# Batching a kernel's 16-bit low products over three blocks of tokens, with the convolution cut by block

## The chip, the cores and the metric

The program runs on one core of a Trainium2 chip. A core has a matrix engine (TensorE, PE in the profile, with its weight loads shown apart as PEld), three further engines (VectorE or DVE, ScalarE or ACT, GpSimd or POOL), a queue that only issues transfers (SyncE or SP), and 16 DMA engines that carry the transfers of all queues. The metric is the device time of one execution in microseconds (us); a number of executions is summed up by its median.

## The reference

An input of 8 sequences of 4096 tokens with 192 features is convolved along the tokens, causally, with 7 taps; the taps are a softmax over 7 weights of each of 8 heads, and a head owns 24 features. The result goes through a two-layer network with a squared ReLU:

```python
w = np.exp(weight - np.max(weight, axis=-1, keepdims=True))
w = w / (np.sum(w, axis=-1, keepdims=True) + 1e-09)           # 8 heads x 7 taps
out = np.einsum('hk,bskhg->bshg', w, x_unf)                    # x_unf: the last 7 tokens
x = out.reshape(32768, 192)
h = x @ w_in                                                   # 192 -> 2048
r = np.maximum(h, 0.0)
g = s * (r * r) + b
return (g @ w_out).astype(np.float32)                          # 2048 -> 192
```

All is float32.

## The kernel before

**Tiling.** The 32768 tokens are 32 super-blocks `n` of 1024 tokens, each of two blocks `j` of 512. The hidden layer of 2048 is 8 pairs `p` of 2 x 128. One step is `(n, j, p)`; there are 16 steps to a super-block. The 192 features are cut into features A (the first 128) and features B (the other 64). The 64 rows of features B of both blocks of a super-block lie above each other in one tile of 128 rows, so one convolution of 512 columns serves both blocks.

**Precision.** TensorE multiplies in a rounded 32-bit format, so every operand is held as a high part and a low part, and the products high x high, low x high and high x low are summed. For convolved features the parts are the two halves of `sA` (features A) and the rows of `tB` (features B). `wA` and `wB` hold the same rows with the upper and lower 64 exchanged; each is made by two DMAs on the SP queue (`swap`, L254 to L258), so that two products on 64 rows each can run side by side on the 128 rows of the array.

**One step on TensorE.** `first(n, j, p)` (L659 to L677) makes 18 products of 64 rows, in pairs, into a PSUM tile `h`: six with `sA`, six with `tB` and `wB`, and last six with `wA`. ScalarE applies ReLU (L684) and squares (L691), VectorE rounds the square to `qh` (L693), and subtracts to get the low part, for `n >= 3` scaled and in 16 bits (`half_lows`, L720 to L729). `second(n, j, p)` then makes the 12 products of `qh` with the output weights. `second` runs two steps behind `first` (LAG), and one more for the first pair of a block; so `second(n, j, 7)`, which ends a block, comes after `first` of step 1 of the next block.

**The low products.** The 16-bit low parts are not multiplied step by step. They wait in a ring of places (`place`, RING = 18 of them) and are multiplied when a block ends. For features A (L829) that is done at the end of every block, on 64 rows, two side by side. For features B (`lows_B`, L783) each product uses 128 rows and 64 columns, two side by side on different columns. They are done for two blocks at once: at the end of a block with `j = 0` they are held, and at the end of `j = 1` the held block's go into a fresh PSUM tile `late` (out of the pool of `h`), the other's into its accumulator. VectorE then adds `late` to the held output tile `oH` (L867).

**Outputs.** At the end of a block ScalarE empties four accumulators into `oA`, `oA2`, `oB`, `oB2` (L843, L846). The rest are DMAs on the POOL queue, in its order: `oB2` is added to `oB` (L858), `oA2` to `oA` (L859), the lower rows of each finished `oB` to its upper rows (L872), and the results go to memory (L875). Each of these waits for the landing of the one that it builds on.

**The convolution ahead.** VectorE convolves features with one instruction a tap (L247 for the first, L249 for the other six), as a list of steps that a generator yields: 7 taps of A for block 0, two of splitting (the ScalarE copy L264; the subtraction L266 with the swap), 7 taps of B, three of splitting B, then A for block 1: 28 steps a super-block. `convolve(k)` advances it by k steps at the end of a step, as the tables CONV and PARTS say. `scale` (L222) sets the taps of a super-block from the peak of its inputs: VectorE reduces (L171, L178, L180, L181), GpSimd multiplies the taps (L228). It is called at the last step of a super-block for the one after the next.

**What sets the order.** The instructions of a step are traced in the order above. A scheduling layer places them on each engine's queue and adds the semaphores; each queue then runs in its order.

## Time and profile before

| what | value |
|---|---|
| median of 3 runs (lowest, highest) | 2040.69 us (2040.59, 2041.22) |
| profiled execution: its own time, its span | 2040.5 us, 2038.6 us |
| PE, busy share of the span | 100%, 18404 products |
| PEld, DVE, ACT, POOL, busy share | 80%, 82%, 65%, 18% |
| mean granted TensorE clock | 1.000 |
| DMA, mean rate | 75 GB/s |

The span runs from the first instruction to the last; the 1.9 us between it and the execution's own time lie around it. A share is an average over the whole span: the first 93 us (super-block 0, with the weights unpacked on the side) differ from the rest. In a timeline row the columns are start in us, duration in us, engine, source line, operation, written tile<-read tiles, shape, count, and in brackets the idle time before it with what ended it. Several products of one kind stand in one row, and since they overlap in pairs, a row's duration runs past the start of the next; distances are read from start to start.

### The profile page before, as it was taken

The numbers are of one execution on the slowest core, as the hardware profiler recorded it, in microseconds if no ns is written. First come the engines' busy times: TensorE is split into PE (matmuls) and PEld (weight loads), VectorE is DVE, ScalarE is ACT, GpSimd is POOL, SyncE is SP. The second block draws the span as 40 slices with busy tenths as digits, with TensorE's granted clock in tenths as the row PEclk, the third lists the DMA queues.
The fourth block names the chain that finished last, engine by engine and source line by source line (L and its number), as shares of the span: only waits on it lengthen the run. The fifth ranks groups of instructions, "written<-read, shape, count | busy, mean of one in ns | idle before, by whom it ended". The sixth has DMA issues, their size and how long they took to land.

```text
span 2038.6 us, 43011 instructions
## 1 busy us (share of the span) xinstructions
PE 2029.5 (100%) x18404; PEld 1632.9 (80%) x18404; DVE 1676.4 (82%) x2232; ACT 1329.8 (65%) x1444; POOL 372.3 (18%) x471
## 2 busy tenths in 40 slices
PE   9999999999999999999999999999999999999999
PEld 6788887877877878778778788787787787887876
DVE  9888988878888878888788888788887888887864
ACT  8878866666666666666666666666666666666665
POOL 0012121112221112211122211122112122112210
PEclk9999999999999999999999999999999999999999
DMA  5023332233332323332333323233323333332321
GB/s 197 21 53 92 79 87 71 64 76 79 81 76 71 71 68 81 84 74 60 73 82 86 76 71 68 71 81 81 74 63 73 81 87 72 73 68 68 71 63 30
DMA packets 60080, 152.82 MB, mean 75 GB/s; under 512 B 11120, under 2 KB 11376, under 8 KB 59888
## 3 DMA queue, kind: packets, MB, share of 16 engines
q0 software_dynamic: 32160, 66.90, 16.1%
q1 hardware_dynamic: 27584, 83.04, 15.2%
q8 instruction: 144, 2.36, 0.6%
q14 instruction: 48, 0.39, 0.2%
q10 hardware_dynamic: 144, 0.13, 0.0%
HBM read 35.57 MB, written 25.20 MB: 30 GB/s over the span
## 4 chain that ended last, share of the span: by engine, by line
PE 96%; DVE 3%; ACT 0%; issue 0%; DMA 0%; SPq 0%; DVEq 0%
PE h L669 47%; PE acc L803 33%; PE acc L829 10%; PE acc L783 3%; PE h L783 3%; DVE ql L698 1%; DVE c L415 0%; DVE t L401 0%; DVE accA L249 0%; DVE W L421 0%; DVE t L398 0%; DVE W L423 0%; DVE t L394 0%; DVE c L414 0%; DMA xA<-in_xA 0%
## 5 line engine op out<-in xcount | busy, mean ns | idle before, releaser
L684 ACT ACTIVATE q<-h 128x1024 f32<-128x1024 f32 x496 | 506.7, 1022 | 415.5 <-PE h L669 414.6
L693 DVE CAST qh<-q 128x1024 fp32r<-128x1024 f32 x477 | 330.1, 692 | 304.1 <-ACT q L691 297.6
L691 ACT ACTIVATE q<-q 128x1024 f32<-128x1024 f32 x512 | 543.8, 1062 | 14.2
L803 PE MATMUL acc<-qh,W 64*128 64x512 f32 x3960 | 513.5, 376 | 0.0
L669 PE MATMUL h<-sA,W 64*128 64x512 f32 x3072 | 427.5, 384 | 2.6 <-DVE W L423 1.7
L803 PEld LDWEIGHTS acc<-qh,W 64*128 64x128 f32 x3960 | 374.9, 186 | 52.5
L669 PE MATMUL h<-wA,W 64*128 64x512 f32 x3072 | 415.6, 376 | 0.0
L669 PE MATMUL h<-wB,W 64*128 64x512 f32 x1536 | 413.6, 376 | 0.0
L669 PE MATMUL h<-tB,W 64*128 64x512 f32 x1536 | 413.6, 376 | 0.0
L726 DVE TENSOR_TENSOR ql<-q,qh 128x1024 f16<-128x1024 f32 x260 | 328.8, 1265 | 9.0
L669 PEld LDWEIGHTS h<-sA,W 64*128 64x128 f32 x3072 | 290.5, 186 | 52.0 <-DVE W L423 2.5
L669 PEld LDWEIGHTS h<-wA,W 64*128 64x128 f32 x3072 | 291.1, 186 | 40.8
L669 PEld LDWEIGHTS h<-tB,W 64*128 64x128 f32 x1536 | 285.4, 186 | 27.3 <-issue 0.2
L803 PE MATMUL acc<-qh,WB 64*128 64x512 f32 x1980 | 299.9, 376 | 0.0
L669 PEld LDWEIGHTS h<-wB,W 64*128 64x128 f32 x1536 | 285.4, 186 | 13.6
L249 DVE SCALAR_TENSOR_TENSOR accA<-xA,taps,accA 128x512 f32<-128x512 f32 x348 | 261.0, 750 | 6.2
L803 PEld LDWEIGHTS acc<-qh,WB 64*128 64x128 f32 x1980 | 187.4, 186 | 26.2
L726 DVE TENSOR_TENSOR words<-q,qh 128x1024 f16<-128x1024 f32 x154 | 194.7, 1264 | 5.3
L829 PEld LDWEIGHTS <-words 64*128 64x128 f16 x1852 | 85.5, 94 | 115.0 <-issue 19.1
L858 POOL DMA_DIRECT2D oB<-oB x60 | 61.6, 1026 | 538.9 <-ACT oB L846 514.0
L249 DVE SCALAR_TENSOR_TENSOR accB<-xB,taps,accB 128x512 f32<-128x512 f32 x174 | 129.9, 747 | 2.2
L843 ACT ACTIVATE oA<-acc,bias,v 128x512 f32<-128x512 f32 x57 | 44.5, 781 | 123.4 <-PE acc L829 123.4
(169 smaller groups left out, 1687.1 us busy)
## 6 DMA issues: line engine op xcount, KB each, us to landing
wA<-sA SPq DMA_DIRECT2D x126, 256.0 KB, 3.7
wB<-tB SPq DMA_DIRECT2D x60, 256.0 KB, 5.1
oB<-oB POOLq DMA_DIRECT2D x60, 256.0 KB, 3.3
oA<-oA POOLq DMA_DIRECT2D x60, 256.0 KB, 3.7
outT<-oA POOLq DMA_DIRECT2D x60, 256.0 KB, 2.3
xA<-in_xA SPq DMA_DIRECT2D x24, 515.0 KB, 3.6
xB<-in_xB SPq DMA_DIRECT2D x32, 259.0 KB, 2.8
oB<-oB POOLq DMA_DIRECT2D x60, 128.0 KB, 2.7
```

What stands on the lines that cost most here:

```text
L249: nc.vector.scalar_tensor_tensor(acc, src, w[:, k : k + 1], acc, op0=ALU.mult, op1=ALU.add)
L669: nc.tensor.matmul(h[:, i, :], w_in(w, p, chunk[0], rows), folded(chunk[part]), start=start, stop=stop,)
L684: nc.scalar.activation(q, h, AF.Relu, scale=scale)
L691: nc.scalar.activation(q, q, AF.Square)
L693: cast(qh, q)
L698: nc.vector.tensor_tensor(ql, q, qh.bitcast(F32), op=ALU.subtract)
L726: nc.vector.tensor_tensor(ql.rearrange("p f (b a) -> p f b a", a=2), *(v.rearrange("p f (a b) -> p f b a", a=2) for v in (q, qh.bitcast(F3 ...
L783: nc.tensor.matmul(to[k * DB :][0:DB], halves[1][:, 2 * p + k, :], ql[:, k, :], start=start and p == 0, stop=p == NPAIR - 1, skip_group_ch ...
L803: nc.tensor.matmul(accs[to + 2 * i], w(f, r), folded(q[r, f % 2, :]), start=start and f == 0, stop=stop and f == ends[i],)
L829: nc.tensor.matmul(accs[2 * i], halves[0][r, f, :], low[r], start=False, stop=f == ends[i],)
L843: nc.scalar.activation(o[k], accs[k], AF.Identity, scale=sb, bias=0.0 if early else bias[:, k : k + 1])
L858: nc.gpsimd.dma_start(o[1], o[3], accum_op=ALU.add)
```

## The change

- `BATCH = 3`: low products of features B are held for two blocks and done at the end of the third, counted over all scaled blocks, whether `j` is 0 or 1. Both halves of `late` are used, for two held blocks, and VectorE adds both (L867 before, L903 in the changed file).
- `RING = 26`: eight more places, in a tile `more` of their own.
- To make room: `sA` and `wA` have two buffers, not three. `tB` and `wB` become one tile for each block (`tB0`, `tB1`, `wB0`, `wB1`), each with one buffer, not two.
- The convolution's steps from super-block 2 on come block by block (`steps_by_block`): B (7 taps and the rounding), then for each block A (7 taps), `split_B` of that block with its own swap, and `split_A`. There are 28 steps as before. Block 0 is `begun` after 18.
- `scale` is called for super-block `n + 1` at step `(n, 0, 2)`, not for `n + 2` at `(n, 1, 7)`.
- PARTS has a row for blocks that start a batch and one for others; the first super-blocks have a table BEGIN.

The diff, without the places that only follow a new name:

```diff
@@ -28,14 +28,28 @@
 WARM = (BLK, BLK // 2, BLK // 2)
-GAP = 136
+GAP = 128
 SCALED = 3
-RING = 18
-PARTS = (1, 5, 2, 1, 1, 2, 1, 1), (2, 3, 0, 2, 1, 2, 2, 2)
+RING = 26
+BATCH = 3
+PARTS = (
+    ((2, 3, 3, 1, 2, 2, 1, 1), (2, 4, 0, 2, 1, 2, 1, 1)),
+    ((1, 4, 3, 2, 1, 2, 1, 1), (1, 7, 0, 1, 1, 1, 1, 1)),
+)
+BEGIN = {
+    (1, 0): (3,) * 8,
+    (1, 1): (1,) * 8,
+    (2, 0): (2, 1, 2, 2, 1, 2, 1, 2),
+    (2, 1): (2, 2, 2, 2, 2, 1, 1, 1),
+    (3, 0): (2, 2, 2, 2, 2, 2, 2, 1),
+    (3, 1): (2, 2, 2, 2, 2, 2, 1, 0),
+}
 EXPONENT = 0x7F800000
...
@@ -222,7 +236,7 @@
             m = greatest(self.peaks, 1)
-            v = small.tile([P, 3], F32, name="v")
+            v = small.tile([P, 3], F32, name="v", bufs=4)
             powers(m, v[:, 0:1], v[:, 1:2], -40)
@@ -259,8 +273,8 @@
         def split_A(self, j, acc):
-            s = self.sA[j] = xs.tile([P, 2, BLK], F32R, name="sA", bufs=3)
-            self.wA[j] = xs.tile([P, 2, BLK], F32R, name="wA", bufs=3)
+            s = self.sA[j] = xs.tile([P, 2, BLK], F32R, name="sA", bufs=2)
+            self.wA[j] = xs.tile([P, 2, BLK], F32R, name="wA", bufs=2)
             nc.scalar.copy(s[:, 0, :], acc)
@@ -269,42 +283,38 @@
             yield
-        def split_B(self, acc):
-            self.tB = xs.tile([P, 2, BLK], F32R, name="tB")
-            self.wB = xs.tile([P, 2, BLK], F32R, name="wB")
-            hiB = xs.tile([P, BLK], F32R, name="hiB", bufs=1)
-            nc.vector.tensor_copy(hiB, acc)
-            yield
-            for j in range(2):
-                r = slice(j * DB, (j + 1) * DB)
-                nc.vector.tensor_copy(self.tB[0:DB, j, :], acc[r, :])
-                nc.vector.tensor_tensor(
-                    self.tB[DB:P, j, :], acc[r, :], hiB[r, :].bitcast(F32), op=ALU.subtract
-                )
-                if j == 1:
-                    self.swap(self.wB, self.tB)
-                    self.begun = True
-                yield
+        def places_B(self, j):
+            self.tB[j] = xs.tile([P, BLK], F32R, name=f"tB{j}", bufs=1)
+            self.wB[j] = xs.tile([P, BLK], F32R, name=f"wB{j}", bufs=1)
+            return self.tB[j], self.wB[j]
+        def split_B(self, j, acc, hiB):
+            r = slice(j * DB, (j + 1) * DB)
+            t, w = self.places_B(j)
+            nc.vector.tensor_copy(t[0:DB, :], acc[r, :])
+            nc.vector.tensor_tensor(
+                t[DB:P, :], acc[r, :], hiB[r, :].bitcast(F32), op=ALU.subtract
+            )
+            self.swap(w, t)
...
@@ -320,14 +330,19 @@
             r = slice(i * HB, (i + 1) * HB)
-            b = (self.tB, self.wB) if i == 0 else (self.wB, self.tB)
+            b = (self.tB[j], self.wB[j]) if i == 0 else (self.wB[j], self.tB[j])
             return (
                 (i, self.sA[j][r, 0, :], self.sA[j][r, 1, :]),
                 (1 - i, self.wA[j][r, 0, :], self.wA[j][r, 1, :]),
-                (2, b[0][r, j, :], b[1][r, j, :]),
+                (2, b[0][r, :], b[1][r, :]),
             )
         def steps(self):
+            if self.n == 1:
+                return self.steps_begin()
+            return self.steps_by_block()
+        def steps_begin(self):
             for j in range(2):
@@ -335,7 +350,27 @@
                     yield from self.conv(acc, self.xB, self.tapB, BLK)
-                    yield from (self.split_B_at_once if self.n == 1 else self.split_B)(acc)
+                    yield from self.split_B_at_once(acc)
+        def steps_by_block(self):
+            accB = xs.tile([P, BLK], F32, name="accB", bufs=1)
+            yield from self.conv(accB, self.xB, self.tapB, BLK)
+            hiB = xs.tile([P, BLK], F32R, name="hiB", bufs=1)
+            nc.vector.tensor_copy(hiB, accB)
+            yield
+            for j in range(2):
+                acc = xs.tile([P, BLK], F32, name="accA")
+                yield from self.conv(acc, self.xA[:, j * BLK :], self.tapA, BLK)
+                self.split_B(j, accB, hiB)
+                yield
+                split = self.split_A(j, acc)
+                next(split)
+                yield
+                next(split)
+                self.begun = True
+                yield
         def conv_tensor(self, acc, diag, x, taps=range(K)):
@@ -709,11 +743,13 @@
                 more = more.rearrange("p k c -> p (k c)")
-            elif k < RING - 2:
+            elif k < 16:
                 more = wordp.tile([P, CT, 2], I32, name="words").bitcast(F16)
                 more = more.rearrange("p f w -> p (f w)")
+            elif k < 18:
+                more = ways[k - 18].bitcast(F16)[:, 4 * P :]
             else:
-                more = ways[k - RING].bitcast(F16)[:, 4 * P :]
+                more = xs.tile([P, (RING - 18) * step], F16, name="more", bufs=1)
             for a in range(0, more.shape[1] - step + 1, step):
@@ -785,10 +821,10 @@
                 )
-    held = {}
-    def holds(n):
-        return SCALED <= n < NSUP - 1
+    held = []
+    def holds(n, j):
+        return n >= SCALED and (n, j) != steps[-1][:2] and (2 * (n - SCALED) + j) % BATCH < BATCH - 1
     def second(n, j, p, qh, ql):
@@ -816,10 +852,11 @@
         if scaled:
-            if p == NPAIR - 1 and j == 1 and holds(n):
-                late = ps_h.tile([P, 2, BLK], F32, name="h")[:, 0, :]
-                lows_B(n, 0, late, range(NPAIR), start=True)
-            if (p == NPAIR - 1 and not (j == 0 and holds(n))) or (n, j, p + 1) == steps[-1]:
+            if (p == NPAIR - 1 and not holds(n, j)) or (n, j, p + 1) == steps[-1]:
+                if held:
+                    late = ps_h.tile([P, 2, BLK], F32, name="h")
+                    for k, block in enumerate(held):
+                        lows_B(*block[0], late[:, k, :], range(NPAIR), start=True)
                 lows_B(n, j, accs[1], range(p + 1))
@@ -858,16 +895,16 @@
                 done = [(toA, o[0])]
-                if j == 0 and holds(n):
-                    held[n] = o[1], toB
+                if holds(n, j):
+                    held.append(((n, j), o[1], toB))
                 else:
                     sums = [(o[1], toB)]
-                    if j == 1 and holds(n):
-                        oH, to = held.pop(n)
+                    for k, (block, oH, to) in enumerate(held):
                         nc.vector.scalar_tensor_tensor(
-                            oH, late, sb, oH, op0=ALU.mult, op1=ALU.add
+                            oH, late[:, k, :], tok_s[block[0]], oH, op0=ALU.mult, op1=ALU.add
                         )
-                        sums.insert(0, (oH, to))
+                        sums.insert(k, (oH, to))
+                    held.clear()
                     for s, to in sums:
@@ -1057,19 +1094,18 @@
             queue.append((n, j, p, *low))
-        if j == 1 and p == NPAIR - 1 and n + 2 in ahead:
+        if (j, p) == (0, 2) and SCALED <= n + 1 < NSUP:
             with behind(nc.vector):
-                ahead[n + 2].scale()
+                tok[n + 1].scale()
         if (n, j) == (1, 1):
             if p < NPAIR - 1:
                 with behind(nc.vector):
                     column_sums(p + 1)
-            convolve(1)
-        elif n > SCALED:
-            convolve(PARTS[j][p])
-        elif p < NPAIR - 1 or n == 1:
-            convolve(3 if n == 1 else 3 - p % 2 if (n, j) == (2, 1) else 2)
+        if (n, j) in BEGIN:
+            convolve(BEGIN[n, j][p])
+        else:
+            batched = (2 * (n - SCALED) + j) % BATCH == 0
+            convolve(PARTS[batched][j][p])
         if (n, j, p) == (2, 0, 0):
```

Line numbers move by 14 to 37: L249, L266, L867, L858, L859, L872, L875 and L228 of the kernel before are L263, L280, L903, L895, L896, L909, L912 and L242 of the changed one.

How the order moves is shown at three places.

**GpSimd's queue where a block with `j = 1` ends a batch.** Before, over the end of block (5, 1), which is worked off at step (6, 0, 1); `v` and `taps` are what `scale` and `unscale` write:

```order
L238 TENSOR_TENSOR v_5022<-v_5022 128x1
L228 TENSOR_SCALAR taps_5026<-tap_58,v_5022,scales_67 128x14
L239 TENSOR_SCALAR v_5022<-v_5022,scales_67 128x1
L203 MEMSET xA_5449 128x6
L872 DMA oB_4772<-oB_4772 64x512
L858 DMA oB_5192<-oB2_5193 128x512
L875 DMA outT<-oB_4772 64x512
L872 DMA oB_5192<-oB_5192 64x512
L875 DMA outT<-oB_5192 64x512
L859 DMA oA_5196<-oA2_5197 128x512
L875 DMA outT<-oA_5196 128x512
```

With the change, at the same place:

```order
L909 DMA oB_4383<-oB_4383 64x512
L909 DMA oB_4769<-oB_4769 64x512
L895 DMA oB_5188<-oB2_5189 128x512
L912 DMA outT<-oB_4383 64x512
L912 DMA outT<-oB_4769 64x512
L909 DMA oB_5188<-oB_5188 64x512
L912 DMA outT<-oB_5188 64x512
L896 DMA oA_5192<-oA2_5193 128x512
L912 DMA outT<-oA_5192 128x512
L252 TENSOR_TENSOR v_5234<-v_5234 128x1
L242 TENSOR_SCALAR taps_5238<-tap_58,v_5234,scales_67 128x14
```

There are two more transfers for the second held block, and the taps stand behind all the block's transfers, where they stood ahead of them.

**VectorE over steps (6, 0, 1) to (6, 0, 3).** Before, from the low part of step 1 to the rounding of step 3:

```order
L726 TENSOR_TENSOR words_3362<-q_5103,qh_5106 128x1024
L247 TENSOR_SCALAR accA_5109<-xA_4659,taps_5026 128x512
L867 SCALAR_TENSOR_TENSOR oB_4772<-h_5127,v_3443,oB_4772 128x512
L249 SCALAR_TENSOR_TENSOR accA_5109<-xA_4659,taps_5026,accA_5109 128x512 x4
L693 CAST qh_5230<-q_5227 128x1024
L726 TENSOR_TENSOR words_3362<-q_5227,qh_5230 128x1024
L249 SCALAR_TENSOR_TENSOR accA_5109<-xA_4659,taps_5026,accA_5109 128x512 x2
L693 CAST qh_5257<-q_5254 128x1024
```

With the change, first what stands between the low part of step 1 and the rounding of step 2:

```order
L762 TENSOR_TENSOR more_3604<-q_5086,qh_5089 128x1024
L263 SCALAR_TENSOR_TENSOR accA_4939<-xA_3839,taps_4425,accA_4939 128x512 x3
L903 SCALAR_TENSOR_TENSOR oB_4383<-h_5107,v_2832,oB_4383 128x512
L903 SCALAR_TENSOR_TENSOR oB_4769<-h_5107,v_3608,oB_4769 128x512
L727 CAST qh_5229<-q_5226 128x1024
```

and then from the low part of step 2 to the rounding of step 3:

```order
L762 TENSOR_TENSOR more_3604<-q_5226,qh_5229 128x1024
L185 TENSOR_REDUCE m_5232<-t_2195 128x1
L192 TENSOR_SCALAR m_5232<-m_5232 128x1
L194 TENSOR_SCALAR v_5234<-m_5232 128x1
L195 TENSOR_SCALAR v_5234<-m_5232 128x1
L295 CAST tB1_5240<-accB_4439 64x512
L296 TENSOR_TENSOR tB1_5240<-accB_4439,hiB_4636 64x512
L280 TENSOR_TENSOR sA_5246<-accA_4939,sA_5246 128x512
L261 TENSOR_SCALAR accB_5252<-xB_4653,taps_5238 128x512
L727 CAST qh_5276<-q_5273 128x1024
```

The row L261 reads `taps_5238`, which GpSimd's row L242 above writes, and the rounding of step 3 stands behind it. The rounding of a step is what `second` of that step waits for.

**VectorE where features A of the next super-block's block 0 are split.** Before, at step (6, 0, 4), twelve steps ahead of their use at (7, 0, 0):

```order
L693 CAST qh_5313<-q_5310 128x1024
L726 TENSOR_TENSOR t_1469<-q_5310,qh_5313 128x1024
L266 TENSOR_TENSOR sA_5260<-accA_5109,sA_5260 128x512
L693 CAST qh_5353<-q_5350 128x1024
L726 TENSOR_TENSOR t_2194<-q_5350,qh_5353 128x1024
```

With the change, at step (6, 1, 5), three steps ahead of their use at (7, 0, 0):

```order
L727 CAST qh_5747<-q_5744 128x1024
L762 TENSOR_TENSOR ql_3107<-q_5744,qh_5747 128x1024
L280 TENSOR_TENSOR sA_5710<-accA_5495,sA_5710 128x512
L261 TENSOR_SCALAR accA_5753<-xA_4652,taps_5238 128x512
L727 CAST qh_5789<-q_5786 128x1024
```

The splitting (L266 before, L280 now) issues the two DMAs that make `wA`. In super-blocks with `n % 3 = 1` it stands one step earlier, at (n, 1, 4).

More of the change, by code (lines that the diff above doesn't have):

```diff
@@ L190, in __init__ @@
             self.tapA, self.tapB, self.s = tapA, tapB, sb
-            self.sA, self.wA = {}, {}
+            self.sA, self.wA, self.tB, self.wB = {}, {}, {}, {}
             self.todo = self.steps() if n else iter(())
@@ L297, in split_B_at_once @@
                 r = slice(j * DB, (j + 1) * DB)
-                places = (self.tB, self.wB) if j == 0 else (self.tB,)
+                t, w = self.places_B(j)
+                places = (t, w) if j == 0 else (t,)
                 for k, to in enumerate(places):
-                    nc.scalar.copy(to[k * DB :][0:DB, j, :], hiB[r, :].bitcast(F32))
+                    nc.scalar.copy(to[k * DB :][0:DB, :], hiB[r, :].bitcast(F32))
                 for k, to in enumerate(places):
                     nc.vector.tensor_tensor(
-                        to[(1 - k) * DB :][0:DB, j, :], acc[r, :], hiB[r, :].bitcast(F32),
+                        to[(1 - k) * DB :][0:DB, :], acc[r, :], hiB[r, :].bitcast(F32),
                         op=ALU.subtract,
@@ L306, in split_B_at_once @@
                 if j == 1:
-                    self.swap(self.wB[:, 1, :], self.tB[:, 1, :])
+                    self.swap(w, t)
                 self.begun = True
@@ L500, in head @@
         w0.his()
-        tB = one.tB = xs.tile([P, 2, BLK], F32R, name="tB")
-        wB = one.wB = xs.tile([P, 2, BLK], F32R, name="wB")
+        (tB0, wB0), (tB1, wB1) = (one.places_B(j) for j in range(2))
         hiB = xs.tile([P, BLK], F32R, name="hiB", bufs=1)
@@ L510, in head @@
         w1.top()
-        nc.scalar.copy(tB[top, 0, :], hiB[top].bitcast(F32))
-        nc.scalar.copy(wB[bottom, 0, :], hiB[top].bitcast(F32))
-        lo(tB[bottom, 0, :], top)
-        lo(wB[top, 0, :], top)
+        nc.scalar.copy(tB0[top, :], hiB[top].bitcast(F32))
+        nc.scalar.copy(wB0[bottom, :], hiB[top].bitcast(F32))
+        lo(tB0[bottom, :], top)
+        lo(wB0[top, :], top)
         w1.his()
@@ L519, in head @@
         w1.los()
-        nc.scalar.copy(tB[top, 1, :], hiB[bottom].bitcast(F32))
+        nc.scalar.copy(tB1[top, :], hiB[bottom].bitcast(F32))
         def second_block():
-            sA = one.sA[1] = xs.tile([P, 2, BLK], F32R, name="sA", bufs=3)
-            wA = one.wA[1] = xs.tile([P, 2, BLK], F32R, name="wA", bufs=3)
+            sA = one.sA[1] = xs.tile([P, 2, BLK], F32R, name="sA", bufs=2)
+            wA = one.wA[1] = xs.tile([P, 2, BLK], F32R, name="wA", bufs=2)
             lo1 = one.split_tensor(acc1, sA[:, 0, :])
             one.swap(wA[:, 0, :], sA[:, 0, :])
-            lo(tB[bottom, 1, :], bottom)
-            one.swap(wB[:, 1, :], tB[:, 1, :])
+            lo(tB1[bottom, :], bottom)
+            one.swap(wB1, tB1)
             lo1(sA[:, 1, :], slice(0, P))
```

2 lines of the change are left out of this document (removed).

## The prediction

> **What bounds the kernel now.** The page first, for the busy shares and the chain that ended last.
>
> ```profile
> span 2038.6 us, 43011 instructions
> PE 2029.5 (100%) x18404; PEld 1632.9 (80%) x18404; DVE 1676.4 (82%) x2232; ACT 1329.8 (65%) x1444; POOL 372.3 (18%) x471
> PE 96%; DVE 3%; ACT 0%; issue 0%; DMA 0%; SPq 0%; DVEq 0%
> ```
>
> Then busy time by stretches, for the steady part (columns: stretch, its length, busy time of PE, PEld, DVE, ACT and POOL with instructions, clock, DMA share, GB/s).
>
> ```profile
> 253.00:2034.00 1781.00, 1780.95 (x16424) 1427.22 (x16420) 1449.87 (x1877) 1123.37 (x1195) 344.61 (x426) 1.00 0.32 73
> ```
>
> Over 1781 us PE is idle for 0.05 us. So TensorE sets the time, and there is no wait left to remove: a gain can only come out of the time between products, and every wait that the change makes costs its full length. What the change needs is therefore a reading of slack. For that I take TensorE's timeline at step (6, 0, 1), where low products end a batch, and, as the last two rows, at (4, 1, 1), where features A's are done alone.
>
> ```profile
> 406.48 1.03 PE L803 MATMUL acc<-qh,W 64*128 64x512 f32 x8
> 407.44 0.62 PE L783 MATMUL h<-words 128*64 128x512 f16 x4
> ...
> 411.01 2.76 PE L829 MATMUL acc<-ql,words 64*128 64x512 f16 x24
> ...
> 414.29 1.00 PE L669 MATMUL h<-sA,W 64*128 64x512 f32 x6
> ...
> 420.95 0.81 PE L669 MATMUL h<-sA,W 64*128 64x512 f32 x6
> ...
> 422.25 0.81 PE L669 MATMUL h<-wA,W 64*128 64x512 f32 x6
> ...
> 426.13 0.59 PE L803 MATMUL acc<-qh,WB 64*128 64x512 f32 x4
> ...
> 427.43 0.81 PE L669 MATMUL h<-sA,W 64*128 64x512 f32 x6
> ...
> 314.71 1.03 PE L803 MATMUL acc<-qh,W 64*128 64x512 f32 x8
> 315.58 1.04 PE L829 MATMUL acc<-t,words 64*128 64x512 f16 x8
> ```
>
> A pair of products takes 0.216 us (six pairs of `first` from 420.95 to 422.25). A step takes 3.24 us (two from 420.95 to 427.43).
>
> **The batches: what is saved.** Four pairs after 406.48 the next should start at 407.34; it starts at 407.44, 0.10 late. From there 16 pairs should take 3.46 us and take 3.57, 0.11 more. At 314.71 the products of features A follow directly, and four pairs take 0.87 us, as they should. A batch of 128 x 64 products thus costs 0.21 us beside its products, whatever its length. Their number goes from 30 (one for each of super-blocks 3 to 30, two at the end) to 20 (57 blocks in threes, and the last). No product goes. Saved: 10 x 0.21 = **2.1 us**.
>
> The Trainium skill ("TensorEngine Tiling (Array Packing)", Key Properties) says that changing the tiling mode drains the engine, and "TensorE: Matmul & The Clock Gate", Single matmul latency, gives some 0.17 us for a drain. By these pages an estimate is two drains or 0.34 us a batch, 3.4 us in all; the trace shows less, and its 0.21 stands.
>
> **The batches: what is added.** Ten more additions of `late` on VectorE (0.74 us each by L867 below). `late` holds one of the two `h` buffers until both additions are done, and `first` of step 3 wants that buffer. A batch is one block longer (8 pairs, 1.73 us), so `first` of step 2 starts at 414.29 + 1.73 = 416.0 and that of step 3 nine pairs later, near 418. The additions are done by 414.5 (worked out below), so this is covered with 3.5 us to spare; without that cover each us would count 19 times.
>
> **The taps behind the transfers.** This is the first wait that I expect. At a batch that ends with `j = 1`, GpSimd's queue now has the taps behind ten transfers, and VectorE's first tap of features B at (n, 0, 2) reads them; behind it on VectorE stands the rounding of step 3, and TensorE's `second` of step 3 waits for that. GpSimd's timeline, this place before:
>
> ```profile
> 404.93 0.69 POOL L238 TENSOR_TENSOR v<-v 128x1 f32<-128x1 f32 x1 [4.78 <-DVE v L181]
> 405.62 0.79 POOL L228 TENSOR_SCALAR taps<-tap,v,scales 128x14 f32<-128x14 f32 x1
> ...
> 412.17 0.89 POOL L872 DMA_DIRECT2D oB<-oB  x1 [3.93 <-DVE oB L867]
> 412.76 1.24 POOL L858 DMA_DIRECT2D oB<-oB  x1
> 415.17 0.59 POOL L875 DMA_DIRECT2D outT<-oB  x1 [1.17 <-DMA oB<-oB]
> 416.60 0.82 POOL L872 DMA_DIRECT2D oB<-oB  x1 [0.84 <-DMA oB<-oB]
> 419.49 0.57 POOL L875 DMA_DIRECT2D outT<-oB  x1 [2.07 <-DMA oB<-oB]
> 420.05 0.91 POOL L859 DMA_DIRECT2D oA<-oA  x1
> 423.87 0.60 POOL L875 DMA_DIRECT2D outT<-oA  x1 [2.91 <-DMA oA<-oA]
> ```
>
> and VectorE's, with the splitting of features B at 453.56 for its duration:
>
> ```profile
> 404.07 0.40 DVE L171 TENSOR_REDUCE m<-t 128x1 f32<-128x256 f32 x1
> ...
> 404.82 0.74 DVE L249 SCALAR_TENSOR_TENSOR accA<-xA,taps,accA 128x512 f32<-128x512 f32 x1
> ...
> 410.73 0.48 DVE L247 TENSOR_SCALAR accA<-xA,taps 128x512 f32<-128x512 f32 x1
> 411.12 0.74 DVE L867 SCALAR_TENSOR_TENSOR oB<-h,v,oB 128x512 f32<-128x512 f32 x1
> 411.79 3.10 DVE L249 SCALAR_TENSOR_TENSOR accA<-xA,taps,accA 128x512 f32<-128x512 f32 x4
> 418.77 0.69 DVE L693 CAST qh<-q 128x1024 fp32r<-128x1024 f32 x1 [3.88 <-ACT q L691]
> ...
> 420.69 1.54 DVE L249 SCALAR_TENSOR_TENSOR accA<-xA,taps,accA 128x512 f32<-128x512 f32 x2
> ...
> 453.56 0.42 DVE L281 CAST tB<-accB 64x512 fp32r<-64x512 f32 x1
> ...
> 454.74 0.49 DVE L247 TENSOR_SCALAR accA<-xA,taps 128x512 f32<-128x512 f32 x1
> ```
>
> I lay the change's order on this clock. VectorE: three taps from 410.73 (0.77 each, as at 411.79) end at 413.1, the two additions at 413.8 and 414.5. GpSimd starts 0.3 after an addition ends (411.86 to 412.17): 414.1, 414.8; the block's own `oB` 0.6 later, 415.4. From here the steps are those of the rows: 3.84 to its summing (412.76 to 416.60), 2.89 to its output (to 419.49), 0.56 to `oA`, 3.82 to that one's output, 0.60 for it, 0.69 and 0.79 for `v` and taps. That gives 428.6. VectorE: the rounding of step 2 comes 1.73 later than at 418.77, its low part ends 1.92 after (420.69), at 422.4; the reduction chain takes 0.75 (404.07 to 404.82), splitting B 1.18 (453.56 to 454.74), splitting A 0.60 (L266 in the third part). It stands ready for the tap at 424.9 and waits till 428.6. The tap takes 0.40, the rounding 0.69: 429.7. TensorE's `second` of step 3 is due at 426.13 + 1.73 = 427.86. It waits 1.8 us, and starts again with a first pair 0.1 slower, as here:
>
> ```profile
> 97.65 0.48 PE L803 MATMUL acc<-ql,WB 64*128 64x512 f32 x2 [0.45 <-DVE ql L698]
> 97.97 0.38 PE L803 MATMUL acc<-qh,WB 64*128 64x512 f32 x2
> ```
>
> (0.32 to the next pair, not 0.216.) So 1.9 us, at n = 6, 9, ..., 30, nine times: **17.2 us**. Bounds: if transfers overlap more, so that everything from 414.1 on comes 1.4 us earlier, 0.5 each, 4.5; if one lands 1.9 later, 3.9 each, 35. I take the direct sum, since the chain of landings repeats rows one for one. Where the batch ends with `j = 0`, or the block before is held, fewer transfers stand ahead and the taps come in time.
>
> **Features split late.** The second wait. `wA` for (n+1, 0, 0) is now issued after the splitting at (n, 1, 5). The same splitting at (6, 0, 4), VectorE then SP's queue, then what the tile's view says of the two landings at 408.2 and 408.7:
>
> ```profile
> 427.14 0.70 DVE L266 TENSOR_TENSOR sA<-accA,sA 128x512 fp32r<-128x512 f32 x1
> ```
>
> ```profile
> 427.99 0.46 SPq L257 DMA_DIRECT2D wA<-sA  x1
> 428.50 0.59 SPq L258 DMA_DIRECT2D wA<-sA  x1
> ```
>
> ```profile
> DMA to landing us min/median/max: 3.0/3.3/3.7
> ```
>
> The second of a pair takes the 3.7: landed at 432.2, 11.2 us after its step began at 420.95. TensorE wants `wA` three steps and six pairs after the beginning: 9.72 + 1.30 = 11.0. It is 0.2 late, and the restart adds 0.1: 0.3 us. In super-blocks with `n % 3 = 1` the splitting is a step earlier and in time; it is late in n = 5, 6, 8, 9, ..., 29, 30, eighteen times: **5.4 us**. Bounds: 0, if VectorE is a little earlier; 2.0 each if the swap takes the 5.7 us that swaps of features B took in some super-blocks, below.
>
> Narrower buffers, the eight new places and the move of `scale` in super-blocks 1 to 3 I cost at nothing: each buffer's last reader is at least one step ahead of its writer, and in the ring 26 places hold three blocks and two steps, as 18 held two and two. The cover is that step of 3.24 us.
>
> **The sum.** 2040.5 (the profiled execution, span and what lies around it) - 2.1 + 17.2 + 5.4 = 2061.0. That execution lies 0.2 under the median of the runs; the forecast is **2061 us**.
>
> **Rivals.** (a) *Both waits are hidden*, the change does what it saves: 2040.7 - 2.1 = 2038.6. For it: the slacks are small, 1.8 and 0.2 us, against durations that were read from other places. Against it: the taps' chain is late by more than any single row is uncertain. (b) *Only the swap is late*, 2040.5 - 2.1 + 5.4 = 2044: the transfers overlap more than in the rows. Against it: each row's wait names the landing before it. (c) *The swaps of features collide.* Features B have twice as many swaps, and those before were sometimes slow:
>
> ```profile
> wB<-tB SPq DMA_DIRECT2D x60, 256.0 KB, 5.1
> ```
>
> ```profile
> wB<-tB SPq DMA_DIRECT2D x1, 256.0 KB, 5.7
> ```
>
> (the second is the one issued at 516.4, while the peak's transfer was in flight). If half of the eighteen swaps of `wA` take 2.0 us longer, 18 us come on top: 2079. Against it: by then the peak's transfer has landed. The Trainium skill ("DMA: Bandwidth & Descriptors", Issuing engines are not separate DMA queues) says that all queues' transfers interleave on the same 16 DMA engines; its rule is that of (c), and the trace agrees in those slow swaps.
>
> **Numbers.** Both waits, 2050 to 2070: 0.55. (a) 0.23. (b) 0.12. (c) 0.08. Something else that gains more: 0.02. A measurement of this kernel tells 0.2% (4.1 us) from no change. Faster: 0.02, since ten batches cannot give more than 2.1. Same: (a) and half of (b), 0.29. Slower: the rest, 0.69. The range takes in (a): 2037 to 2068; the forecast's own is 2050 to 2070.
>
> **What would show it.** In the changed profile: L783 and its neighbours with ten gaps fewer; VectorE's first tap of `accB` waiting for GpSimd's taps at n = 6, 9, ..., by 3.7 us, and TensorE's `second` of step 3 behind it, waiting for the rounding; TensorE waiting at the first `wA` product of a super-block, named as DMA. TensorE still without idle time would make this wrong and (a) right.

## The result: 2126 us, four times the loss that was predicted

| | before | changed |
|---|---|---|
| median (lowest, highest), us | 2040.7 (2040.2, 2041.9) | 2126.1 (2119.7, 2131.4) |
| profiled execution, its span, us | 2040.5, 2038.6 | 2128.9, 2127.1 |

The ratio is 1.0417, with a 95% interval of 1.0398 to 1.0435: 85.4 us slower, where 20.5 were predicted. From the page of the changed kernel, the span, the busy times and the chain that ended last:

```profile
span 2127.1 us, 43260 instructions
...
PE 2062.7 (97%) x18404; PEld 1649.0 (78%) x18404; DVE 1681.5 (79%) x2242; ACT 1321.7 (62%) x1444; POOL 334.6 (16%) x471
...
PE 77%; DMA 9%; DVE 6%; issue 3%; ACT 3%; POOL 2%; SPq 0%; DVEq 0%; POOLq 0%; ACTq 0%
```

TensorE is no longer the whole chain. Note also that its busy time rose by 33 us (2029.5 before), although it has the same 18404 products: products became slower, and idle time alone is not the answer. Busy time by stretches, the steady part and then 5 us behind a long wait (the third number from the end is the granted clock):

```profile
253.00:2120.00 1867.00, 1812.37 (x16422) 1443.66 (x16422) 1457.38 (x1891) 1115.71 (x1195) 304.18 (x426) 0.99 0.30 70
...
436.00:441.00 5.00, 4.41 (x22) 3.54 (x24) 4.89 (x6) 0.00 (x0) 0.00 (x0) 0.51 0.01 3
```

In those 5 us TensorE ran at half its clock. What stands ahead of them, in TensorE's timeline at step (6, 0, 5):

```profile
430.01 0.81 PE L703 MATMUL h<-wA,W 64*128 64x512 f32 x6
436.60 1.22 PE L839 MATMUL acc<-qh,WB 64*128 64x512 f32 x4 [5.77 <-DVE qh L727]
437.61 1.91 PE L839 MATMUL acc<-qh,W 64*128 64x512 f32 x8
439.32 1.49 PE L703 MATMUL h<-sA,W 64*128 64x512 f32 x6
```

`second` of step 3 waits for the rounding (L727). Four pairs from 437.61 to 439.32 take 1.71 us, 0.427 a pair, where 0.216 is normal. Below, an idle time is the distance between two starts less the normal 0.216: 5.9 us here, a little more than the 5.77 of the row, which counts from the modelled end of a product. VectorE and then GpSimd at the same place:

```profile
427.27 0.69 DVE L280 TENSOR_TENSOR sA<-accA,sA 128x512 fp32r<-128x512 f32 x1
435.45 0.49 DVE L261 TENSOR_SCALAR accB<-xB,taps 128x512 f32<-128x512 f32 x1 [7.49 <-POOL taps L242]
435.86 0.68 DVE L727 CAST qh<-q 128x1024 fp32r<-128x1024 f32 x1
```

```profile
416.81 1.73 POOL L909 DMA_DIRECT2D oB<-oB  x2 [0.80 <-DVE oB L903]
418.01 1.43 POOL L895 DMA_DIRECT2D oB<-oB  x1
421.00 1.24 POOL L912 DMA_DIRECT2D outT<-oB  x2 [1.56 <-DMA oB<-oB]
423.07 1.03 POOL L909 DMA_DIRECT2D oB<-oB  x1 [0.82 <-DMA oB<-oB]
427.59 0.55 POOL L912 DMA_DIRECT2D outT<-oB  x1 [3.49 <-DMA oB<-oB]
428.13 0.93 POOL L896 DMA_DIRECT2D oA<-oA  x1
434.29 0.57 POOL L912 DMA_DIRECT2D outT<-oA  x1 [5.24 <-DMA oA<-oA]
434.88 0.21 POOL L252 TENSOR_TENSOR v<-v 128x1 f32<-128x1 f32 x1
435.06 0.36 POOL L242 TENSOR_SCALAR taps<-tap,v,scales 128x14 f32<-128x14 f32 x1
```

This is the predicted chain, engine by engine. The block as a whole runs 2.6 us later than the prediction's clock (waits at (6, 0, 0) and before), and the first additions are where it put them: 416.8 = 414.1 + 2.7. From there to the taps' end it allowed 14.5 us, and the rows take 18.6. The waits of the whole span (total us, times, longest):

```profile
DVE accB L261 <- POOL taps L242: 62.2, 29, 7.5
...
PEld acc L839 <- DVE qh L727: 46.3, 13, 6.2
...
PE acc L839 <- DVE qh L727: 41.3, 11, 5.8
...
PEld h L703 <- DMA wA<-sA: 24.5, 32, 1.9
...
PE h L703 <- DMA wA<-sA: 12.6, 21, 1.5
```

The first row counts VectorE's waits in all super-blocks, so it is not TensorE's loss, although the next table has a similar number. TensorE's loss can be had exactly, because both kernels run the same 512 steps. I take the start of every `first` (the first row of L703, of L669 before) and compare the distance to the next start in both traces. Everything is in a few places:

| steps | us |
|---|---|
| (n, 0, 5) and (n, 0, 6), n = 6, 9, ..., 30: the taps ("wait 1") | +62.0 |
| (n, 0, 0), the 18 predicted super-blocks: swaps of `wA` ("wait 2") | +21.7 |
| (4, 0, 0): the same, not predicted | +2.0 |
| 0.21 more at 19 batches (below) | +4.0 |
| ahead of super-block 4 | +1.1 |
| ten batches fewer | -2.1 |
| sum (the starts of the last step differ by 88.8) | 88.7 |

Of the 62.0, nine waits are 42.4 (2.8 to 5.9 us each, 4.7 on average), their restarts 0.9, and 18.7 are pairs at half clock, behind eight of the nine (none behind the shortest, at n = 30). Some 1.7 of the 21.7 are half clock too, at (21, 0, 0), where the longest wait for `wA` was followed by it. Wait 2 at its best-seen place, (7, 0, 0): TensorE's row, SP's two rows, what the tile's view says of the landing of these two, and GpSimd just ahead:

```profile
478.35 1.52 PE L703 MATMUL h<-wA,W 64*128 64x512 f32 x6 [0.94 <-DMA wA<-sA]
```

```profile
473.29 0.46 SPq L271 DMA_DIRECT2D wA<-sA  x1
473.80 0.59 SPq L272 DMA_DIRECT2D wA<-sA  x1
```

```profile
DMA to landing us min/median/max: 5.0/5.1/5.1
```

```profile
461.67 0.76 POOL L171 DMA_DIRECT2D there<-peak  x1 [5.28 <-DVE peak L231]
462.42 0.93 POOL L896 DMA_DIRECT2D oA<-oA  x1
470.62 0.75 POOL L177 DMA_DIRECT2D t<-there  x1 [7.27 <-DMA there<-peak]
471.35 0.55 POOL L912 DMA_DIRECT2D outT<-oA  x1
```

The swap took 5.1 us, not 3.7, and two other transfers were in flight when it was issued: the peak's second (470.62) landed at 475.5 and features A's output (471.35) at 476.4. At the eighteen places the second transfer of the swap took 4.7 us on average (3.7 to 5.6, the 14 landings that the trace has). The 0.21 at the batches comes from the same waits: when `wA` lands, the two products of a pair start apart, the pairs are off by one from there on, and the last product before the batch stands alone. It can be seen at 409.50 (five products, an odd number, where the kernel before has even ones):

```profile
409.50 0.81 PE L839 MATMUL acc<-qh,W 64*128 64x512 f32 x5
410.24 0.62 PE L819 MATMUL h<-more,words 128*64 128x512 f16 x4
```

### The profile page after: what moved, and what is told of

It is laid out like the page before. It is cut to its first block, busy times and chain, and to the rows that moved or that the text cites. A ratio compares the mean times of both kernels' runs of the same rounds, so it can differ in the third digit from the quotient of the medians.

```text
span 2127.1 us, 43260 instructions
## 1 busy us (share of the span) xinstructions
PE 2062.7 (97%) x18404; PEld 1649.0 (78%) x18404; DVE 1681.5 (79%) x2242; ACT 1321.7 (62%) x1444; POOL 334.6 (16%) x471
## 4 chain that ended last, share of the span: by engine, by line
PE 77%; DMA 9%; DVE 6%; issue 3%; ACT 3%; POOL 2%; SPq 0%; DVEq 0%; POOLq 0%; ACTq 0%
PE h L703 39%; PE acc L839 27%; PE acc L866 8%; DMA wA<-sA 4%; DMA oA<-oA 3%; DMA oB<-oB 2%; PE h L819 2%; ACT q L725 1%; ACT q L718 1%; DVE accA L263 1%; PE acc L819 1%; POOL outT L912 1%; DVE qh L727 1%; DVE ql L732 1%; POOL oB L909 1%
## 5 line engine op out<-in xcount | busy, mean ns | idle before, releaser
L727 DVE CAST qh<-q 128x1024 fp32r<-128x1024 f32 x477 | 330.5, 693 | 323.8 <-ACT q L725 322.6
L839 PE MATMUL acc<-qh,W 64*128 64x512 f32 x3960 | 545.6, 380 | 0.0
L703 PE MATMUL h<-wA,W 64*128 64x512 f32 x3072 | 447.7, 379 | 13.5 <-DMA wA<-sA 12.6
L703 PE MATMUL h<-sA,W 64*128 64x512 f32 x3072 | 453.3, 387 | 2.6 <-DVE W L458 1.6
L839 PEld LDWEIGHTS acc<-qh,W 64*128 64x128 f32 x3960 | 400.9, 188 | 54.9
L703 PE MATMUL h<-wB,W 64*128 64x512 f32 x1536 | 412.4, 379 | 0.2 <-DMA wB<-tB 0.2
L703 PE MATMUL h<-tB,W 64*128 64x512 f32 x1536 | 412.4, 379 | 0.0
L839 PE MATMUL acc<-qh,WB 64*128 64x512 f32 x1980 | 330.2, 382 | 41.3 <-DVE qh L727 41.3
L703 PEld LDWEIGHTS h<-wA,W 64*128 64x128 f32 x3072 | 312.3, 187 | 65.6 <-DMA wA<-sA 24.5
L703 PEld LDWEIGHTS h<-sA,W 64*128 64x128 f32 x3072 | 312.0, 188 | 52.9 <-DVE W L458 2.4
L703 PEld LDWEIGHTS h<-tB,W 64*128 64x128 f32 x1536 | 270.2, 188 | 25.6 <-issue 0.2
L703 PEld LDWEIGHTS h<-wB,W 64*128 64x128 f32 x1536 | 270.2, 188 | 17.2 <-DMA wB<-tB 0.6
L839 PEld LDWEIGHTS acc<-qh,WB 64*128 64x128 f32 x1980 | 209.6, 188 | 72.0 <-DVE qh L727 46.3
L263 DVE SCALAR_TENSOR_TENSOR accA<-xA,taps,accA 128x512 f32<-128x512 f32 x348 | 260.5, 749 | 5.8
L762 DVE TENSOR_TENSOR ql<-q,qh 128x1024 f16<-128x1024 f32 x180 | 226.6, 1259 | 6.2
L762 DVE TENSOR_TENSOR more<-q,qh 128x1024 f16<-128x1024 f32 x140 | 176.1, 1258 | 4.8
L895 POOL DMA_DIRECT2D oB<-oB x60 | 60.2, 1004 | 602.5 <-ACT oB L883 600.1
L762 DVE TENSOR_TENSOR words<-q,qh 128x1024 f16<-128x1024 f32 x108 | 135.9, 1258 | 3.7
L263 DVE SCALAR_TENSOR_TENSOR accB<-xB,taps,accB 128x512 f32<-128x512 f32 x174 | 130.1, 748 | 2.1
```

The costliest lines, as they stand in the source:

```text
L263: nc.vector.scalar_tensor_tensor(acc, src, w[:, k : k + 1], acc, op0=ALU.mult, op1=ALU.add)
L703: nc.tensor.matmul(h[:, i, :], w_in(w, p, chunk[0], rows), folded(chunk[part]), start=start, stop=stop,)
L727: cast(qh, q)
L762: nc.vector.tensor_tensor(ql.rearrange("p f (b a) -> p f b a", a=2), *(v.rearrange("p f (a b) -> p f b a", a=2) for v in (q, qh.bitcast(F3 ...
L839: nc.tensor.matmul(accs[to + 2 * i], w(f, r), folded(q[r, f % 2, :]), start=start and f == 0, stop=stop and f == ends[i],)
L895: nc.gpsimd.dma_start(o[1], o[3], accum_op=ALU.add)
```

## The experiments

The kernels below start from the changed one. For each, the two waits were summed by step starts as above, over its profiled execution:

| kernel | median us | wait 1 | wait 2 (n, 0, 0) |
|---|---|---|---|
| changed | 2126.1 | 62.0 | 23.6 |
| taps' first use two steps later | 2075.4 | 8.0 | 23.2 |
| `scale` at its old place | 2060.3 | 0.0 | 20.3 |
| features A split a step earlier | 2096.1 | 54.6 | 2.4 |
| peak a step earlier | 2107.2 | 54.9 | 11.9 |
| swap two steps later | 2065.7 (one run) | 0.8 | 20.9 |
| `scale` back and split earlier | 2039.5 | 0.0 | 0.1 |

**1. The taps' first use two steps later.**

```diff
-    ((1, 4, 3, 2, 1, 2, 1, 1), (1, 7, 0, 1, 1, 1, 1, 1)),
+    ((1, 4, 2, 0, 4, 2, 1, 1), (1, 7, 0, 1, 1, 1, 1, 1)),
```

> The changed kernel, but where a block with j = 0 starts a batch, VectorE's first tap of features B comes after step 4, not after step 2 (a row of PARTS: 1, 4, 2, 0, 4, 2, 1, 1). GpSimd's order and all transfers stay. Theory: all that TensorE loses at (n, 0, 5) and (n, 0, 6), 62.0 us over n = 6, 9, ..., 30, is the tap waiting for GpSimd and the clock that falls behind the wait; the rounding of step 5 has two steps more, 6.5 us, against waits of at most 5.9. So the time is 2126 - 62 = 2064 us, the clock 1.00 there, and the waits at the first products with wA stay. Rival: something else on VectorE or GpSimd is behind the taps (the additions of late, the new transfers), and a later wait takes the place of this one: above 2100.

Measured: 2075.4 us (2069.0 to 2075.9), ratio 1.0163 (1.0148 to 1.0179). At (n, 0, 5) and (n, 0, 6) nothing is left, but 8.0 us came back at (n, 0, 7) and (n, 1, 0) of n = 6, 12 and 21 (0.1 at 27). VectorE at step (6, 0, 4):

```profile
435.95 0.49 DVE L261 TENSOR_SCALAR accB<-xB,taps 128x512 f32<-128x512 f32 x1 [4.12 <-POOL taps L242]
436.48 2.33 DVE L263 SCALAR_TENSOR_TENSOR accB<-xB,taps,accB 128x512 f32<-128x512 f32 x3
438.72 0.69 DVE L727 CAST qh<-q 128x1024 fp32r<-128x1024 f32 x1
```

Its four taps stand in one step, and the rounding follows 2.77 us after the taps come, not 0.4. I had counted the 6.5 us of two steps as free and forgotten the three taps that I put there. Some 51 us went, of the 62 expected. So the wait did go with the taps; an eighth of it came back as the rival's later wait, by my own placing of the taps.

**2. `scale` at its old place.**

```diff
-        if (j, p) == (0, 2) and SCALED <= n + 1 < NSUP:
+        if j == 1 and p == NPAIR - 1 and n + 2 in ahead:
             with behind(nc.vector):
-                tok[n + 1].scale()
+                ahead[n + 2].scale()
```

> One part of the change undone: the taps of a super-block are set at the last step of the super-block two before it, as in the kernel before, so GpSimd makes them ahead of the batch's transfers. VectorE's order is otherwise the changed one, its first tap of features B after step 2 included. Theory: as with the later tap, 2064 us; the place of the taps in GpSimd's queue alone makes the wait. Rival: VectorE itself is late there (four steps of the convolution behind one low part): then the rounding of step 3 still comes late, and some 20 us or more of the 62 stay, above 2080.

Measured: 2060.3 us (2059.9 to 2063.8), ratio 1.0096 (1.0079 to 1.0113). Wait 1 is 0.0 at every n; of the waits on TensorE over 1 us in the sum, that for `wA` alone belongs to the steady part:

```profile
PE h L703 <- DMA wA<-sA: 10.5, 18, 1.7
```

The VectorE rival is out: with the same four convolution steps in that place the rounding is in time. The place of the taps in GpSimd's queue made the wait.

**3. Features A split one step earlier.**

```diff
-    ((2, 3, 3, 1, 2, 2, 1, 1), (2, 4, 0, 2, 1, 2, 1, 1)),
+    ((2, 3, 3, 1, 2, 2, 1, 1), (2, 4, 1, 2, 2, 1, 0, 1)),
```

> The changed kernel, but features A of the next block 0 are split one step earlier in the two of three super-blocks where they were late (a row of PARTS: 2, 4, 1, 2, 2, 1, 0, 1), so at (n, 1, 4) everywhere. The taps stay as they are. Theory: TensorE loses 27.8 us to swaps of wA that land late, 2.0 of it at n = 4, which this doesn't touch; with 3.24 us more no other is late: 2126 - 25.6 = 2100 us. Rival: the transfers that the swaps collide with (the peak's, features A's output) stand just ahead of them, and a swap that starts earlier only meets more of them: a gain of less than 10 us, above 2116.

Measured: 2096.1 us (2095.3 to 2103.2), ratio 1.0280 (1.0263 to 1.0297). Of the 23.6 at (n, 0, 0), 2.4 stay (1.8 at n = 4, 0.6 at n = 9), and batches go back to their old length where the pairs stay together. Some 5 us of the 30 are not from wait 2: wait 1 was shorter in this profile, by 7 us, which lies within the 12 us over which the executions of the changed kernel spread.

**4. The peak one step earlier.**

```diff
-            elif p == 2:
+            elif p == 1:
                 with behind(nc.vector):
                     ahead[n + 2].peak()
```

> The changed kernel, but the peak of the inputs two super-blocks ahead is taken at step (n, 1, 1), not (n, 1, 2), so its two transfers (3.2 us apart from their old place) are over before the swap of wA at (n, 1, 5). Theory: a swap of wA lands in 3.7 to 3.8 us when it is alone and in 5.1 when the peak's second transfer is in flight, which is why the waits at (n, 0, 0) are 1.2 us and not the 0.3 of the prediction: of 27.8 us some 16 to 20 go, so about 2108 us. Rival: the swap is late by VectorE or by SP's own queue, and the peak has no part in it: no change, 2126.

Measured: 2107.2 us (2104.4 to 2109.8), ratio 1.0326 (1.0311 to 1.0342). Wait 2 halves, 23.6 to 11.9; the rest of the 19 us is in wait 1, again shorter in this profile, so the match with 2108 is better than the reason deserves. The second transfer of the swap took 4.1 us on average at the eighteen places (4.7 before), and the one at (6, 1, 5) 4.4, with features A's output still in flight. The peak's second transfer is one cause of the long swaps, not the only one. Why it was in flight at all shows on VectorE at (n, 1, 1): the changed table puts four taps ahead of the peak's reduction.

```profile
456.53 3.11 DVE L263 SCALAR_TENSOR_TENSOR accA<-xA,taps,accA 128x512 f32<-128x512 f32 x4
459.55 1.22 DVE L231 TENSOR_REDUCE peak<-xA 128x1 f32<-128x1030 f32 x1
```

The kernel before had one there:

```profile
443.85 0.74 DVE L249 SCALAR_TENSOR_TENSOR accB<-xB,taps,accB 128x512 f32<-128x512 f32 x1
444.51 1.22 DVE L217 TENSOR_REDUCE peak<-xA 128x1 f32<-128x1030 f32 x1
```

Three taps are 2.3 us, and the peak's transfers leave that much later in the super-block. Counted from the start of block (6, 1), the second landed at 26.0 us in the kernel before and at 28.9 with the change, where the swap is issued at 26.7.

**5. The swap two steps later, where a block with `j = 0` starts a batch.**

```diff
-    ((1, 4, 3, 2, 1, 2, 1, 1), (1, 7, 0, 1, 1, 1, 1, 1)),
+    ((1, 4, 0, 0, 4, 3, 2, 1), (1, 7, 0, 1, 1, 1, 1, 1)),
```

> The changed kernel, but where a block with j = 0 starts a batch, splitting features A of block 1 and its swap of wA come after step 4, not after step 2 (a row of PARTS: 1, 4, 0, 0, 4, 3, 2, 1), with the first two taps of features B behind it. What is disputed is why a chain of transfers that the prediction put at 1.8 us of lateness was late by 2.8 to 5.9 us at n = 6, 9, ..., 30. Theory: features A's accumulation (oA) meets the swap of features A that is issued in the same moment; in these nine places its landing took 4.6 to 6.6 us, and takes 3.3 to 3.7 when the swap comes 6 us later. No wait at (n, 0, 5) is left, and the time is about 2064 us. Rival: the landing is long by its place behind three other transfers on GpSimd's queue, whatever SP does: 4.6 us or more still.

Measured in one execution: 2065.7 us, and wait 1 is 0.8. That wait says nothing about the landings, since the row also puts the first tap behind the rounding of step 3, as in experiment 1. What the view of line L896 says of the landing of features A's accumulation issued at 428.13 in the changed kernel:

```profile
DMA to landing us min/median/max: 5.9/5.9/5.9
```

and of the one issued at 428.31 here:

```profile
DMA to landing us min/median/max: 3.3/3.3/3.3
```

Over the nine places the time from this issue to features A's output fell from 5.9 to 4.4 us on average (3.8 in the prediction), and the whole chain from the first addition to the taps from 17.4 to 16.2. The five landings that both traces show are 5.9, 6.6, 5.8, 4.9 and 4.6 us in the changed kernel, and 3.3, 4.2, 4.0, 4.2 and 3.5 here. So the swap made the landing long, and not the place in the queue. VectorE didn't: in the changed kernel it stood idle from 427.96 to 435.45, through the whole landing. The 4.4 is still not 3.8; swaps of features B were in flight there in both kernels, and no run takes them away.

**6. The price of a wait by its length.** The base is the kernel of experiment 7.

```diff
+            some = [n for n in range(4, NSUP) if n % 3]
+            again = 6 + 7 * some.index(self.n) % 18 if j == 1 and self.n in some else 0
+            for _ in range(1 + again):
-            nc.vector.tensor_copy(t[0:DB, :], acc[r, :])
+                nc.vector.tensor_copy(t[0:DB, :], acc[r, :])
```

> The kernel without both waits, into which waits of rising length are put, to read the price of a wait by its length: at step (n, 0, 2) of the 18 super-blocks with n % 3 = 1 or 2 from 4 to 29, and of 31, VectorE copies one part of tB1 6 to 23 times more than once, in mixed order, and the rounding of step 3 stands behind. Theory: TensorE's second of step 3 waits for 0 to 7 us; a wait costs its length and 0.1 us up to some length, and from there 1 to 2.7 us more, because TensorE's clock falls to half behind it (pairs at 427 ns) until the next point of a grid of 3.41 us. By the waits so far, 3.69 and 3.78 us stayed free in some places and 1.6 us did not in others, so no sharp length is expected: the share of waits with a slow stretch rises from none below 1.5 us to all above 4. Rival: a fixed length decides.

Measured in one execution: 2128.8 us. The copies came between VectorE's other work, so that TensorE waited at `second` of step 4, one step behind the place that was expected; its idle time is read there. The cost beyond it is what steps (n, 0, 3) to (n, 1, 7) took longer than without the copies, less the idle time:

| idle us | cost beyond it, us |
|---|---|
| 0.53, 0.98, 1.45, 1.91, 2.38, 2.79, 3.28 | 0.32 to 0.34 each |
| 3.72 | 1.92 |
| 4.19, 4.64 | 1.79, 1.79 |
| 5.10 | 3.01 |
| 5.59 to 6.00 (six) | 1.68 to 2.94 |

The 0.3 are the restart and two more of 0.1 at later steps. The granted clock behind the waits of 3.28, 4.19 and 5.10 us, by stretches:

```profile
368.70:372.10 3.40, 3.16 (x30) 2.77 (x30) 3.33 (x5) 0.00 (x0) 0.00 (x0) 1.00 0.02 5
1159.10:1162.50 3.40, 3.38 (x16) 2.73 (x18) 3.33 (x5) 0.00 (x0) 0.00 (x0) 0.53 0.00 0
1949.00:1953.00 4.00, 4.00 (x20) 3.16 (x20) 3.93 (x5) 0.00 (x0) 0.00 (x0) 0.50 0.00 0
```

Nothing was changed here but the length of a wait, so the half clock is the wait's doing. Within this run a length between 3.3 and 3.7 would decide, as the rival has it. Over all kernels of this study it doesn't: of 87 idle times of 0.45 to 1.6 us none was followed by half clock, of 12 between 1.6 and 3.6 five were, of 7 between 3.6 and 3.85 five (3.69 and one of 3.78 were not), and all 26 that were longer.

**7. Both waits away.** `scale` as in experiment 2, the split as in 3, and super-block 3's table:

```diff
-    (3, 1): (2, 2, 2, 2, 2, 2, 1, 0),
+    (3, 1): (3, 3, 2, 2, 2, 1, 0, 0),
```

> Both waits taken away at once: the taps set at the last step two super-blocks before, as in the kernel before, features A of the next block 0 split one step earlier, and the same in super-block 3 (BEGIN (3, 1): 3, 3, 2, 2, 2, 1, 0, 0). Batches of three blocks and the ring of 26 stay. Theory: nothing else in the change costs time, so the ten batches less show: 2040.4 - 2.1, and 0.5 to 1 us that super-block 3 still loses: 2039 us, between 2038.3 and 2040. Rival: narrower buffers and twice as many swaps have a price of their own that the two waits covered: 2042 or more.

Measured: 2039.45 us (2038.7 to 2040.9; before on the same chip 2040.8), ratio 0.9994 (0.9985 to 1.0003). TensorE is back where it was, 0.76 us idle in 1781 by the busy times:

```profile
253.00:2034.00 1781.00, 1780.24 (x16434) 1432.21 (x16432) 1458.27 (x1895) 1119.25 (x1196) 337.90 (x426) 1.00 0.31 73
```

By step starts every place but the batches is within 0.1 us of the kernel before, from super-block 4 on, in this profile. In a second profile of the same kernel, taken for experiment 8, two swaps were again late, by 0.4 us at n = 4 and 0.3 at n = 9: one step more is just enough. Buffers, ring and twice as many swaps cost TensorE nothing. Against the kernel before the time can't be told from no change.

**8. Batches of two in that kernel.** Two versions. The first, with `BATCH` alone changed, leaves features B of block (31, 0) unwritten; the second does the last super-block as the kernel before, and ran beside the kernel of experiment 7 once more.

```diff
-BATCH = 3
+BATCH = 2
...
-        return n >= SCALED and (n, j) != steps[-1][:2] and (2 * (n - SCALED) + j) % BATCH < BATCH - 1
+        return SCALED <= n < NSUP - 1 and (2 * (n - SCALED) + j) % BATCH < BATCH - 1
```

> The same kernel with BATCH = 2: batches end with every super-block, as in the kernel before; all else stays the changed one. It measures the gain of the batch alone. Theory: 30 batches again, at 0.21 us each, so 2.1 us more than with three blocks, 2041 us. Rival: a batch is free at its edges, or the longer batch costs elsewhere what it saves: no difference over 0.5 us.

> The kernel without both waits once more, beside the next one on the same chip, for their difference: 2039.4 us, as before.

> The kernel without both waits, with batches of two blocks as in the kernel before, and the last super-block's two blocks done one by one as there, so that all outputs are written (the kernel with BATCH = 2 ahead of this one leaves the features B of block (31, 0) unwritten). Theory: the 30 batches of the kernel before at 0.21 us each, so 2.1 us above the kernel with batches of three, and equal to the kernel before within 0.5 us. Rival: the gain of the batch is eaten by something that came with the batch of three: both kernels equal.

Measured: the first 2040.9 us, which is not used, since it does less than the whole work; then 2039.8 with batches of three (ratio to the kernel before 0.9994, 0.9985 to 1.0004) and 2041.9 with batches of two (1.0005, 0.9996 to 1.0014). The difference of the two medians is 2.1 us, as expected, with intervals that overlap. The step starts are sharper: in the profile of experiment 7 the steps with batches gained 1.9 us, and one pair at n = 12 fell apart for 0.21; the sum of both is ten times 0.21. In the second profile they gained 1.7, with two pairs apart.

## Why the prediction was wrong

- **What bounds the kernel**: right. With the waits gone TensorE is the bound again, and each us of wait had cost its full length, and more.
- **The batches, saved and added**: right, 2.1 us, and nothing lost to the two additions of `late`. The estimate of 3.4 us from the Trainium skill ("TensorEngine Tiling (Array Packing)", Key Properties, a drain at each change of mode) was too high, and the row's 0.21 a batch held.
- **The taps behind the transfers**: right in mechanism, place, engines and count (nine), wrong in size: 62.0 us, not 17.2. Two terms failed. (The "ten transfers" ahead of the taps are nine by the order shown; the sum doesn't use the number.)
  - *The chain of landings* was taken row by row from a place where the transfers met hardly any others. From the first addition to the taps' end it was 14.5 us in the prediction and 17.4 on average over the nine. From its own accumulation to its summing features B took 4.9 instead of 3.84, with the held blocks' two outputs between; from there to its output 3.4 instead of 2.89; features A's accumulation 5.9 instead of 3.82; the taps themselves 1 us less than their rows. The net 2.9 makes the wait 4.7 where it was put at 1.8. The reason "the chain of landings repeats rows one for one" did not hold, since the change moves swaps of features A and B into these microseconds: experiment 5 takes one swap out, and the landing is 3.3 again. Experiment 5 accounts for 1.5 of the 2.9; what lengthened features B's transfers wasn't isolated. The upper bound (one landing 1.9 later, 35 us) was too near for the same reason: one landing alone was 2.1 later, and others came on top.
  - *The half clock* behind the wait has no term in the sum at all: 18.7 us over eight waits. The kernel before had no row to price it from: starts 0.43 us apart stand only in its first 17 us, and behind those its longest idle times, of 1.1 us, have none after them. Whether it would have come at the predicted idle of 1.8 is open: of the four waits of 1.6 to 2.0 us in all traces, three were followed by it. At the 4.7 that the first error hid it was nearly certain.
- **Features split late**: right in mechanism and in all 18 places but one of little size (n = 31, 0.1 us), wrong in size: 21.7 us and 3.8 of split pairs, not 5.4. The swap's landing was taken as 3.7 us, and was 5.1 at n = 7 and 4.7 on average. VectorE's and SP's part held: the swap left 7.55 us into its step at n = 7, as forecast. This is rival (c), which had a chance of 0.08. Its price, 18 us more, is near what came partly by luck: it took half of the swaps as 2.0 us longer, and nearly all were longer, by 1.0 on average. Its dismissal, "by then the peak's transfer has landed", is the step that failed: the change's own table delays the peak by three taps, and with it the landing from just ahead of the swap to 2.2 us behind its issue (experiment 4). That (4, 0, 0) waits too was missed.
- **The parts at nothing**: right for buffers and ring (experiment 7). Wrong for one that was not listed: the order of taps and peak at (n, 1, 1).
- **Range**: 2037 to 2068 took both bounds from undisturbed landings, and had no room for the clock. It was also narrower than the prediction's own upper bounds, 35 us for the taps and 2.0 for each of eighteen swaps, which add up to 2109; the measured time lies above that too. The direction was right, and so were the rows named to look for: all of them are in the profile after, the waits with larger numbers.
- The Trainium skill's rule named under (c) ("DMA: Bandwidth & Descriptors", Issuing engines are not separate DMA queues) agrees with experiment 5: a swap on SP's queue lengthened an accumulation on GpSimd's from 3.3 to 5.9 us.

## What to carry to other kernels

A landing time read from a quiet place is a lower bound: before it is used, lay out what else the change puts into the same microseconds, and give each transfer a second price with company (here, for features A's accumulation, 3.3 us nearly alone, 4.6 to 8.2 in most of the changed kernel). On an engine that is never idle a forecast wait of several us has a second price behind it, since the clock fell behind all but one of the nine here, so an error in a wait's length is not linear in time. Where an order is written as a table, check everything that shares a step with a moved row, the peak here, and not only the row.

## What was not expected of the hardware

**The end of half clock lies on a grid.** In the changed kernel the nine slow stretches (eight behind the taps, one at (21, 0, 0)) end at 440.8, 638.5, 836.9 us and so on; divided by a period of 3.413 us the nine ends leave remainders between 0.49 and 0.88, over 1382 us, while their beginnings leave anything from 0.0 to 3.2. In the run with doses, 3.413 us is again the period that fits best (ten ends, remainders 1.98 to 2.44). So a wait's extra cost, 1.05 to 2.74 us by excess of slow pairs, depends on how far off the next point is. The Trainium skill ("TensorE: Matmul & The Clock Gate", Part 1: The HAM clock gate) states a free-running window of 3413 ns, and these ends agree. Its practical rule, no idle gaps above some 3.4 us (HAM oscillation), agrees only roughly: in five cases idle times of 1.6 to 2.9 us were enough, and 3.69 and 3.78 once each were not. What decides between them was not settled.

**Large transfers behind a small one landed late.** The peak's first transfer moves 1 KB and lands in 8.6 us (columns: transfer, queue, count, KB each, median us to landing):

```profile
there<-peak POOLq DMA_DIRECT2D x29, 1.0 KB, 8.6
```

Features A's accumulations issued in its company, 0.8 us after it, landed in 7.4 to 8.2 us in the changed kernel, 3.2 to 3.5 when nearly alone. They are part of the reason why the median went from 3.7 to 6.2: before, they came after the peak's second transfer in GpSimd's queue. No wait of TensorE hung on these. Experiment 4 puts them behind the second transfer again, and the median falls only to 5.4, with six of 60 still at 7.1 to 8.1. So that the small transfer is the cause is argued from the times, and not shown.

**A wait can cost 0.21 us long after it.** When one product of a pair starts before its partner's data are there, the pairing stays off by one until the next change of shape, where a product stands alone.
